# One level of Strassen's scheme in the second layer of a fused retention and feed-forward kernel

## Chip, cores and metric

The kernel runs on one core of one Trainium2 chip. Times are device microseconds of one execution. Compared runs come from the same chip, and from the same rounds, with one exception: of the seven runs of before beside e9 to e12, six are listed by the record with e1 to e4 too, so only the comparisons of e9 to e12 with each other are wholly of one call. An execution more than 1.5% above the fastest of its kernel is called slow and left out of ratios. Engines: PE is TensorE, PEld its weight loads, DVE VectorE, ACT ScalarE, POOL GpSimd.

## The reference

```python
# q, k, v: (8, 8, 576, 64)   w_in: (512, 2048)   w_out: (2048, 512), all float32
scores = (q @ k^T) / sqrt(64)
gamma  = 1 - 2 ** (-5 - arange(8))                   # per head
ret    = (scores * D) @ v     # D[i, j] = gamma ** (i - j) if i >= j else 0
x      = ret.transpose(0, 2, 1, 3).reshape(4608, 512)
h      = x @ w_in
out    = maximum(0.01 * h, h) @ w_out                # (4608, 512) float32
```

## The kernel before

Retention runs in units of up to 128 tokens, one "step" per unit: scores, outputs of the unit before, masks, states. The feed-forward part runs in token groups, three of 256, seven of 512, one of 256. `run` interleaves the first layer of group g with the second layer of group g-1 and puts the steps between their blocks. Every engine executes its instructions in the order of these calls.

```python
    def steady(n):
        def go():
            ...
            scores(n)                 # PE
            outputs(n - 1)            # PE, then ACT copy "own", then DVE sums into xT
            masks(n)                  # DVE
            states(n)                 # DVE, then POOL cast of the states
            casts(n + 2)              # ACT k, POOL q and v, DMA transpose
    ...
    def g2_blocks(g, width=1):        # second layer, 64 products of 512 columns per 512 tokens
        ...
            for f in range(4 * part, 4 * part + 4):
                for tb in tbs:
                    nc.tensor.matmul(out=y_cur[g, tb],
                        lhsT=g_tiles[g][:, f, tb * P : (tb + 1) * P],
                        rhs=w_out16[:, f, :], start=(f == 0), stop=(f == NF - 1))
            if part == 3:             # DVE copy to SBUF, then DMA out
        ...
    def run(upto, *lists):
        order = sorted(((n + 0.5) / len(ls), x, n)
                       for x, ls in enumerate(lists) for n in range(len(ls)))
        a = done
        for m, (_, x, n) in enumerate(order):
            lists[x][n]()
            run_steps(min(upto, a + -(-(upto - a) * (m + 1) // max(1, len(order) - 3)), done + 1))
        run_steps(upto)
    ...
    run(ends[3], g1[2] + g2_blocks(2))
    run(ends[4], g1_blocks(3))
    for g in range(4, NG):
        run(ends[g + 1], g1_blocks(g), g2_blocks(g - 1))
    run(ends[NG], g2_blocks(NG - 1))
```

## Time and profile before

| | before |
|---|---|
| median of its first three runs | 337.44 us (335.61 to 338.17) |
| span of the profiled run, granted clock | 337.3 us, 0.973 |
| PE, DVE, ACT, POOL busy | 299.5, 147.8, 135.6, 122.0 us |

Two rows of the groups by cost, from the page of the kernel before. The columns are busy us and mean ns of one instruction, then the idle time of the engine before them and what ended it.

```profile
L451 PE MATMUL yps<-w_out,gt 128*128 128x512 f16 x512 | 127.9, 379 | 0.0
L461 DVE COPY osb<-yps 128x512 f32<-128x512 f32 x32 | 21.9, 687 | 69.9 <-PE yps L451 69.9
```

The second layer's PE work never waits (0.0), and DVE spends most of its time before these copies idle. The mean of 379 ns is a pipelined duration; the pace is read start to start.

### The profile page before, as it was taken

What the parts mean: (1) busy time and instruction counts of PE and PEld (TensorE: products, weight loads), DVE (VectorE), ACT (ScalarE), POOL (GpSimd) and SP (SyncE); (2) the same over time, 40 slices, a digit from 0 to 9 for tenths busy, and PEclk for the clock granted to TensorE, in tenths of its full rate; (3) what the DMA queues carried; (4) which work ended last, traced back from release to release, by engine and by line L of the source; (5) the groups of instructions that cost most, each with busy time, mean ns of one, the idle gap of its engine ahead of it and who ended that gap; (6) DMA issues with size and microseconds to landing.
All of it is one profiled execution on the core that took longest, in us unless ns stands there. A gap on an engine that the chain in (4) does not pass through costs nothing.

```text
span 337.3 us, 8449 instructions
## 1 busy us (share of the span) xinstructions
PE 299.5 (89%) x3578; PEld 154.7 (46%) x3578; DVE 147.8 (44%) x326; ACT 135.6 (40%) x240; POOL 122.0 (36%) x148
## 2 busy tenths in 40 slices
PE   1798887595775699999999999999999999999995
PEld 0476643263332344444444444444444444445652
DVE  2670444945564336434453556354436553101011
ACT  3355631164153454444453545444444433332220
POOL 8786745605355333530540355035413510000000
PEclk9999799989997779999999999999999999999999
DMA  7999999879999986866779599968697211000111
GB/s 175 214 194 189 228 231 178 197 150 176 165 244 198 162 161 142 175 144 165 160 139 192 130 189 210 217 148 158 149 214 109 66 47 61 35 33 31 62 64 62
DMA packets 122982, 50.32 MB, mean 149 GB/s; under 512 B 112192, under 2 KB 116288, under 8 KB 122944
## 3 DMA queue, kind: packets, MB, share of 16 engines
q1 hardware_dynamic: 115632, 37.11, 54.8%
q0 software_dynamic: 7024, 12.59, 19.6%
q8 instruction: 28, 0.46, 0.6%
q10 hardware_dynamic: 288, 0.08, 0.1%
q14 instruction: 10, 0.08, 0.1%
HBM read 36.78 MB, written 9.44 MB: 137 GB/s over the span
## 4 chain that ended last, share of the span: by engine, by line
PE 65%; DMA 13%; issue 10%; POOL 9%; SPq 1%; DVE 0%; POOLq 0%
PE yps L451 31%; PE hps L428 29%; DMA t<-in_v_dram 6%; DMA w_out<-in_moe_w_out_dram 5%; POOL t L122 3%; POOL v L160 2%; POOL qk L140 2%; DMA qkT<-qk 2%; PE sc L201 2%; POOL w_in L343 2%; PE ot L313 1%; PE ot L303 1%; PE sc L211 1%; SPq L122 1%; SPq L148 0%
## 5 line engine op out<-in xcount | busy, mean ns | idle before, releaser
L428 PE MATMUL hps<-xT,w_in 128*128 128x512 f16 (+1 forms) x704 | 151.2, 352 | 3.6 <-DVE osb L505 3.4
L435 ACT ACTIVATE gt<-hps 128x512 f16<-128x512 f32 x144 | 85.6, 596 | 128.0 <-PE hps L428 127.8
L451 PE MATMUL yps<-w_out,gt 128*128 128x512 f16 x512 | 127.9, 379 | 0.0
L428 PEld LDWEIGHTS <-w_in 128*128 128x128 f16 x704 | 68.8, 101 | 62.7 <-issue 9.6
L327 DVE TENSOR_TENSOR xT<-ot,own 64x256 f16<-64x256 f32 (+1 forms) x144 | 50.3, 388 | 85.8 <-ACT own L321 85.3
L451 PEld LDWEIGHTS <-gt 128*128 128x128 f16 x512 | 49.1, 98 | 56.4
L249 POOL CAST st<-s 128x512 f16<-128x512 f32 x25 | 15.3, 610 | 135.3 <-DVE s L243 68.6
L461 DVE COPY osb<-yps 128x512 f32<-128x512 f32 x32 | 21.9, 687 | 69.9 <-PE yps L451 69.9
L321 ACT COPY own<-ot 128x512 f32<-128x512 f32 (+1 forms) x36 | 19.4, 538 | 38.2 <-PE ot L313 34.8
L140 POOL TENSOR_TENSOR qk<-t,cs 128x512 f16<-128x512 f32 (+1 forms) x32 | 33.4, 1043 | 0.1
L160 POOL TENSOR_TENSOR v<-t,cs 128x512 f16<-128x512 f32 (+1 forms) x32 | 33.4, 1042 | 0.0
L221 DVE TENSOR_TENSOR s<-sc,cs 128x512 f16<-128x512 f32 (+1 forms) x40 | 27.5, 689 | 5.0 <-PE sc L211 4.0
L139 ACT CAST qk<-t 128x512 f16<-128x512 f32 (+1 forms) x40 | 24.7, 620 | 7.4 <-DMA t<-in_k_dram 7.4
L201 PE MATMUL sc<-qkT 64*64 64x64 f16 x576 | 13.5, 205 | 14.6 <-DMA qkT<-qk 11.2
L201 PEld LDWEIGHTS <-qkT 64*64 64x64 f16 x576 | 9.0, 113 | 30.5 <-DMA qkT<-qk 17.2
L182 PE MATMUL yps<-ident,qk 128*128 128x128 f16 (+1 forms) x48 | 5.9, 274 | 11.3 <-ACT qk L139 8.4
L140 DVE TENSOR_TENSOR qk<-t,cs 128x512 f16<-128x512 f32 (+1 forms) x8 | 7.9, 986 | 18.0 <-DMA t<-in_q_dram 18.0
L313 PE MATMUL ot<-qkT,st 64*64 64x64 f16 x456 | 11.8, 197 | 2.2 <-ACT st L249 1.6
L303 PE MATMUL ot<-s,v 64*64 64x64 f16 x512 | 11.7, 197 | 0.3 <-DVE s L221 0.3
L122 POOL DMA_DIRECT2D t<-in_q_dram x12 | 10.5, 877 | 3.8 <-DVE qk L140 1.9
L122 POOL DMA_DIRECT2D t<-in_v_dram x12 | 10.2, 851 | 4.3 <-DMA t<-in_k_dram 1.5
L182 PEld LDWEIGHTS <-qk 128*128 128x128 f16 (+1 forms) x56 | 4.4, 119 | 16.1 <-ACT qk L139 11.1
(42 smaller groups left out, 152.8 us busy)
## 6 DMA issues: line engine op xcount, KB each, us to landing
out_dram<-osb SPq DMA_DIRECT2D x36, 256.0 KB, 2.3
t<-in_k_dram SPq DMA_DIRECT2D x23, 256.0 KB, 3.8
t<-in_q_dram SPq DMA_DIRECT2D x22, 256.0 KB, 4.5
t<-in_v_dram SPq DMA_DIRECT2D x22, 256.0 KB, 4.8
t<-in_q_dram POOLq DMA_DIRECT2D x10, 256.0 KB, 7.8
t<-in_v_dram POOLq DMA_DIRECT2D x10, 256.0 KB, 8.2
t<-in_k_dram POOLq DMA_DIRECT2D x9, 256.0 KB, 8.0
w_in<-in_moe_w_in_dram POOLq DMA_DIRECT2D x16, 128.0 KB, 6.0
```

The source lines that it names most:

```text
L122: eng.dma_start(out=t[0:n], in_=(q, k, v)[x][b, :, P * w : P * w + n, :].rearrange("h t d -> t h d"),)
L139: nc.scalar.copy(out=t[0:n, 1], in_=t32[u, 1][0:n])
L140: (nc.vector if u < NEARLY else nc.gpsimd).tensor_tensor(out=t[0:n, 0], in0=t32[u, 0][0:n], in1=tab_sb[0:n, w % 2, 0, :].unsqueeze(2).to_b ...
L160: (nc.vector if u < NEARLY else nc.gpsimd).tensor_tensor(out=t[0:n], in0=t32[u, 2][0:n], in1=tab_sb[0:n, w % 2, 1, :].unsqueeze(2).to_broa ...
L201: nc.tensor.matmul(out=a[half(j), g, 0, p, :], lhsT=qkT[u][half(g), 1, p, half(j)], rhs=qkT[u][half(g), 0, p, half(j)], start=True, stop=T ...
L221: nc.vector.tensor_tensor(out=s16s[u][0:n], in0=sc_tiles[u][0:n, :, 0], in1=mask_sb[0:n].unsqueeze(1).unsqueeze(1).to_broadcast([n, 2, NP, ...
L321: nc.scalar.copy(out=tmp[:, :, 0:nb, :], in_=own[:, 0:nb].rearrange("q j p t -> q p j t"))
L327: nc.vector.tensor_tensor(out=xT[half(o), ps, t0 : t0 + n].rearrange("q p (j t) -> q p j t", t=CH), in0=far[half(o), o ^ c, :, 0:nb, :], i ...
L428: nc.tensor.matmul(out=hps[:, f, :], lhsT=w_in16[:, c, fc * P : (fc + 1) * P], rhs=xT[:, c, t0 % XR : t0 % XR + tok], start=(c == 0), stop ...
L435: nc.scalar.activation(out=g_tiles[g][:, fb * nf : (fb + 1) * nf, :], in_=hps, func=mybir.ActivationFunctionType.Lrelu,)
L451: nc.tensor.matmul(out=y_cur[g, tb], lhsT=g_tiles[g][:, f, tb * P : (tb + 1) * P], rhs=w_out16[:, f, :], start=(f == 0), stop=(f == NF - 1),)
L461: nc.vector.tensor_copy(out=osb, in_=y_cur[g, tb])
```

## The change

The intent is to remove PE work where PE is the bound. A 512 by 2048 by 512 product is cut in two along each dimension. Seven half-size products replace eight, and sums of activations, weights and results are computed instead, all f16 sums on VectorE. Per group: four f16 sums of 2048 elements per partition, 112 products of 256 columns, five PSUM sums on DVE and two copies on ACT. Four weight sums come once.

```diff
+    def mix_weights(eng):
+        pairs = ((w_part(0, 1), w_part(0, 0)), (w_part(1, 1), w_mix[:, 0]),
+                 (w_part(1, 1), w_part(0, 1)), (w_part(1, 0), w_mix[:, 1]))
+        for n, (x, y) in enumerate(pairs):
+            eng.tensor_tensor(out=w_mix[:, n], in0=x, in1=y, op=SUB)
+    def g2_seven(g):
+        ...
+        def mix(n):
+            z, x, y, op = (
+                (s[:, 0], part(1, 0), part(1, 1), ADD),
+                (s[:, 1], s[:, 0], part(0, 0), SUB),
+                (part(1, 0), part(0, 0), part(1, 0), SUB),
+                (part(0, 1), part(0, 1), s[:, 1], SUB),
+            )[n]
+            nc.vector.tensor_tensor(out=z, in0=x, in1=y, op=op)
+        plan = (
+            ("p1", g_(0, 0), w_part(0, 0), True, lambda: keep("k1", "p1")),
+            ("p6", s(1), w_mix[:, 1], True, lambda: keep("u2", "p6", "k1")),
+            ("p1", g_(0, 1), w_part(1, 0), False, lambda: give(0, 0, "p1")),
+            ("p5", s(0), w_mix[:, 0], True, lambda: keep("v", "p5", "u2")),
+            ("p7", g_(1, 0), w_mix[:, 2], True, lambda: give(1, 1, "p7", "v")),
+            ("p5", g_(0, 1), w_part(1, 1), False, lambda: give(0, 1, "p5", "u2")),
+            ("p7", g_(1, 1), w_mix[:, 3], False, lambda: give(1, 0, "p7", "u2")),
+        )
+        def block(n, half):
+            name, lhs, rhs, fresh, then = plan[n]
+            if n == 0 and not half:
+                mix(0)
+                mix(1)
+            if n in (1, 3) and not half:
+                mix((n + 3) // 2)
+            product(name, lhs, rhs, fresh, half)       # 8 products of 256 columns
+            if half:
+                then()                                 # DVE sum or ACT copy out of PSUM
     ...
     run(ends[3], g1[2] + g2_blocks(2))
+    mix_weights(nc.vector)
     run(ends[4], g1_blocks(3))
     for g in range(4, NG):
-        run(ends[g + 1], g1_blocks(g), g2_blocks(g - 1))
+        run(ends[g + 1], g1_blocks(g), g2_seven(g - 1))
```

(Cut: buffers and smaller rings for the retention tiles. The `product`, `keep` and `give` helpers are only named.)

More of the change, by code (lines that the diff above doesn't have):

```diff
@@ L13 @@
 ADD = mybir.AluOpType.add
+SUB = mybir.AluOpType.subtract
 PSUM = bass.MemoryType.PSUM
@@ L73 @@
     a_pool = ctx.enter_context(tc.tile_pool(name="ap", bufs=4))
+    b_pool = ctx.enter_context(tc.tile_pool(name="bp", bufs=2))
     g_pool = ctx.enter_context(tc.tile_pool(name="gp", bufs=2))
     o_pool = ctx.enter_context(tc.tile_pool(name="op", bufs=4))
+    o2_pool = ctx.enter_context(tc.tile_pool(name="op2", bufs=2))
+    s_pool = ctx.enter_context(tc.tile_pool(name="sp", bufs=1))
+    m_pool = ctx.enter_context(tc.tile_pool(name="mp", bufs=1))
     sc_pool = ctx.enter_context(tc.tile_pool(name="scp", bufs=1, space=PSUM))
@@ L219, in masks @@
         n = nrows[u]
-        s16s[u] = a_pool.tile([P, 2, NP, CH], F16, name="s16")
+        s16s[u] = b_pool.tile([P, 2, NP, CH], F16, name="s16")
         nc.vector.tensor_tensor(
@@ L240, in states @@
         else:
-            tmp = a_pool.tile([P, NP, CH], FP, name="stmp")
+            tmp = b_pool.tile([P, NP, CH], FP, name="stmp")
             nc.vector.tensor_tensor(out=tmp, in0=st[:, 1], in1=s32[:, 0], op=ADD)
@@ L319, in outputs @@
         t0 = (b * S + P * w) % XR
-        tmp = a_pool.tile([P, NP, 2, CH], FP, name="own")
+        tmp = b_pool.tile([P, NP, 2, CH], FP, name="own")
         nc.scalar.copy(
@@ L422, in block @@
             if fb == 0:
-                g_tiles[g] = g_pool.tile([P, NF, tok], F16, name=f"gt{tok}")
+                if g == 1:
+                    g_tiles[g] = g_tiles["both"][:, :, tok : 2 * tok]
+                else:
+                    g_tiles["both"] = g_pool.tile([P, NF, TOK], F16, name="gt")
+                    g_tiles[g] = g_tiles["both"][:, :, 0:tok]
             hps = h_pool.tile([P, nf, tok], FP, name="hps")
@@ L469, in g2_blocks, with w_part @@
         ]
+    w_mix = const_pool.tile([P, 4, NF // 2, DM // 2], F16, name="w_mix")
+    HF, HN, HT = NF // 2, DM // 2, TOK // 2
+    def w_part(a, b):
+        return w_out16[:, a * HF : (a + 1) * HF, b * HN : (b + 1) * HN]
+    def mix_weights(eng):
+        pairs = (
+            (w_part(0, 1), w_part(0, 0)),
+            (w_part(1, 1), w_mix[:, 0]),
+            (w_part(1, 1), w_part(0, 1)),
+            (w_part(1, 0), w_mix[:, 1]),
+        )
+        for n, (x, y) in enumerate(pairs):
+            eng.tensor_tensor(out=w_mix[:, n], in0=x, in1=y, op=SUB)
@@ new lines, in g2_seven, with part, product, keep @@
+    def g2_seven(g):
+        t0 = starts[g]
+        gt = g_tiles[g]
+        r = {}
+        def part(a, b):
+            return gt[:, b * HF : (b + 1) * HF, a * HT : (a + 1) * HT]
+        def mix(n):
+            if "s" not in r:
+                r["s"] = s_pool.tile([P, 2, HF, HT], F16, name="mix")
+            s = r["s"]
+            z, x, y, op = (
[5 more added lines that the diff above has]
+            nc.vector.tensor_tensor(out=z, in0=x, in1=y, op=op)
+        def product(name, lhs, rhs, fresh, half):
+            if fresh and not half:
+                r[name] = y_pool.tile([P, 2, HN], FP, name="yps")
+            for f in range(HF // 2 * half, HF // 2 * (half + 1)):
+                for tb in range(2):
+                    nc.tensor.matmul(
+                        out=r[name][:, tb, :],
+                        lhsT=lhs()[:, f, tb * P : (tb + 1) * P],
+                        rhs=rhs[:, f, :],
+                        start=fresh and f == 0 and tb == 0,
+                        stop=f == HF - 1,
+                        skip_group_check=True,
+                    )
+        def keep(name, of, plus=None):
+            r[name] = m_pool.tile([P, 2, HN], FP, name=name)
+            if plus is None:
+                nc.scalar.copy(out=r[name], in_=r[of])
+            else:
+                nc.vector.tensor_tensor(out=r[name], in0=r[of], in1=r[plus], op=ADD)
+        def give(a, b, of, plus=None):
+            if ("o", a) not in r:
+                r["o", a] = o2_pool.tile([P, 2, DM], FP, name="osb2")
+            to = r["o", a][:, :, b * HN : (b + 1) * HN]
+            if plus is None:
+                nc.scalar.copy(out=to, in_=r[of])
+            else:
+                nc.vector.tensor_tensor(out=to, in0=r[of], in1=r[plus], op=ADD)
+            r["n", a] = r.get(("n", a), 0) + 1
+            if r["n", a] == 2:
+                r0 = t0 + a * HT
+                nc.sync.dma_start(
+                    out=out[r0 : r0 + HT, :].rearrange("(t p) d -> p t d", p=P),
+                    in_=r["o", a],
+                )
+        def s(n):
+            return lambda: r["s"][:, n]
+        def g_(a, b):
+            return lambda: part(a, b)
+        plan = (
[6 more added lines that the diff above has]
+            ("p7", g_(1, 1), w_mix[:, 3], False, lambda: give(1, 0, "p7", "u2")),
+        )
+        def block(n, half):
[8 more added lines that the diff above has]
+                then()
+        return [lambda n=n, half=half: block(n, half) for n in range(7) for half in range(2)]
```

## The prediction

> **What bounds the kernel now.** I read the busy table and the 40 slices first, then busy time in stretches, then the instructions in order of time of TensorE (PE), VectorE (DVE) and GpSimd (POOL) round a group boundary.
>
> ```profile
> PE   1798887595775699999999999999999999999995
> PEclk9999799989997779999999999999999999999999
> ```
>
> ```profile
> 80.00:120.00 40.00, 27.23 (x477) 13.16 (x478) 21.74 (x53) 14.85 (x27) 16.86 (x19) 0.89 1.24 193
> 120.00:285.00 165.00, 165.00 (x1975) 78.14 (x1974) 79.96 (x183) 74.80 (x132) 55.62 (x63) 1.00 0.71 148
> ```
>
> The columns of the second view are stretch, length, then busy us of PE, weight load, DVE, ACT, POOL, clock, DMA share, GB/s. From 120 us on PE is never idle, at clock 1.00; DVE is at 80 of 165 us (48%). So a microsecond less of PE work there is a microsecond of span, and a microsecond of new PE waiting costs the same. From 80 to 120 us PE is idle 12.8 us and the bound is a chain of waits. All seven changed second layers lie after about 124 us; the preparation of the weights lies in the chain-bound stage.
>
> The price of the two product shapes is in the last groups, PE in order of time:
>
> ```profile
> 306.35 1.04 PE L428 MATMUL hps<-xT,w_in 128*128 128x256 f16 x8
> 307.22 1.89 PE L451 MATMUL yps<-w_out,gt 128*128 128x512 f16 x8
> 308.95 1.04 PE L428 MATMUL hps<-xT,w_in 128*128 128x256 f16 x8
> ```
>
> Start to start, eight 256-column matmuls take 0.87 us (0.109 each), eight 512-column ones 1.73 us (0.216 each). Halving the columns halves the time: the 98 ns weight load of each still hides.
>
> The second thing to see is how late DVE runs after each retention step (scores, masks, states of one 128-token unit). PE, DVE and POOL at one group boundary:
>
> ```profile
> 153.59 1.03 PE L428 MATMUL hps<-xT,w_in 128*128 128x512 f16 x4
> 154.54 0.32 PE L201 MATMUL sc<-qkT 64*64 64x64 f16 x16
> ...
> 155.19 1.04 PE L451 MATMUL yps<-w_out,gt 128*128 128x512 f16 x4
> ```
>
> ```profile
> 155.96 1.53 DVE L327 TENSOR_TENSOR xT<-ot,own 64x256 f16<-64x256 f32 x4 [1.48 <-ACT own L321]
> 157.52 0.69 DVE L221 TENSOR_TENSOR s<-sc,cs 128x512 f16<-128x512 f32 x1
> ...
> 159.03 0.42 DVE L243 TENSOR_TENSOR s<-stmp,cs 128x256 f32<-128x256 f32 x1
> ```
>
> ```profile
> 159.52 0.61 POOL L249 CAST st<-s 128x512 f16<-128x512 f32 x1 [8.81 <-DVE s L243]
> 160.09 1.04 POOL L140 TENSOR_TENSOR qk<-t,cs 128x512 f16<-128x512 f32 x1
> 161.09 1.04 POOL L160 TENSOR_TENSOR v<-t,cs 128x512 f16<-128x512 f32 x1
> ```
>
> The new group's first first-layer block ends on PE at 154.45 (call it E), the step's 64x64 matmuls end 0.7 later, and DVE is through with the step only at 159.45 = E + 5.0. Then POOL at once starts 2.65 us of back-to-back work. Today nobody waits for this: PE has other blocks.
>
> **What the Trainium skill says.** (1) "TensorE: Matmul & The Clock Gate", section "Wait — 56ns, not 53.3ns?": a warm matmul costs N / 2.4 GHz plus about 2.5 ns; 0.216 and 0.109 us agree. Its section "What's actually happening" says idleness of about 3.4 us halves the clock; the trace agrees in kind (below). (2) "VectorE: DVE Perf Modes", section "The perf-mode tier table (the rule you actually need)": a tensor_tensor of 2048 bf16 elements, all in SBUF, runs at 2x in 1224 ns, at 1x 2293 ns. No DVE sum of two f16 SBUF inputs is in this trace; its f32 sums of 512 take 690 ns. I take 1.22 us as an estimate from that page. (3) "SBUF — State Buffer", section "Who interferes with whom": a DVE instruction with two SBUF inputs and a GpSimd instruction that reads SBUF exclude each other, the later one blocking fully. The trace has one such meeting, and agrees:
>
> ```profile
> 61.80 3.06 DVE L140 TENSOR_TENSOR qk<-t,cs 128x512 f16<-128x512 f32 x1
> 64.78 0.68 DVE L160 TENSOR_TENSOR v<-t,cs 128x512 f16<-128x512 f32 x1
> ```
>
> ```profile
> 61.27 1.04 POOL L160 TENSOR_TENSOR v<-t,cs 128x512 f16<-128x512 f32 x1
> 62.27 1.03 POOL L140 TENSOR_TENSOR qk<-t,cs 64x512 f16<-64x512 f32 x1
> 63.27 1.03 POOL L160 TENSOR_TENSOR v<-t,cs 64x512 f16<-64x512 f32 x1
> ```
>
> A 0.69 us DVE product issued while POOL was busy ended when POOL's whole run of three was over: it took 3.06.
>
> **The change, part by part.** *PE work.* Per group 64 x 0.216 = 13.8 us become 112 x 0.109 = 12.2; 1.65 saved, times seven groups: **-12 us**, all on the path.
>
> *DVE work.* Four f16 sums of 2048 elements (4 x 1.22 = 4.9 us) and five PSUM sums for four copies (about +0.7): +5.6 us on 14 us of each group of some 29 us. DVE goes from 48% to about 67%: not the bound by throughput.
>
> *Where it waits.* The instruction order of the changed kernel (built, not run) puts, at each new group, one first-layer block, one retention step, and then on DVE the first two sums, strictly behind that step's work. The second product reads the second sum, and PE gets to it after the step and four half-blocks: E + 0.7 + 4 x 0.865 = E + 4.2. DVE is free at E + 5.0 when the step's unit has three state sums, E + 4.6 with two, E + 3.7 without states (64-row units). Two dependent sums add 2.5. So PE waits even with no contention: by the five full and two short cases, groups in order 2.9, 3.3, 2.9, 2.9, 2.0, 2.0 us, and the last, which has no step but must wait for the last activation, about 0.8. Sum **+16.8 us**.
>
> *The lock.* In the first four groups POOL is released by the same state sum, and its 2.65 us falls against the two sums. Whoever is first, the second sum depends on the first, so POOL gets in between or ahead, and by the 61.80 case keeps the port until its run ends. +2.65 each, four times: **+10.6 us**. The other groups' steps have no states, so POOL is done by then.
>
> *Weight sums.* Four sums, 4.9 us, once, on DVE ahead of a step at about 94 us, in the stage where PE already waits for DVE:
>
> ```profile
> 98.19 0.32 PE L201 MATMUL sc<-qkT 64*64 64x64 f16 x16 [2.13 <-DVE s L239]
> ```
>
> Each step there is fed by the one before (DVE states, POOL casts, DMA transpose, scores), so a delay is handed on: **+5 us**, less if the transposes catch up.
>
> *Clock.* After such idle stretches the clock sags: after 2.76 us idle the next eight 512-column matmuls took
>
> ```profile
> 105.35 3.10 PE L428 MATMUL hps<-xT,w_in 128*128 128x512 f16 x8
> ```
>
> 3.10 instead of about 1.9 in the same view, 1.2 us lost. Five waits of 5 us or more: up to 6; I put **+3**.
>
> *The rest.* The product buffers are freed by DVE or ACT one product or more before PE needs them; by the same count the third buffer (freed by the sum u2) is ready at about the time PE comes, so 0 to 0.4 us. Two ACT copies (1.2 us per group on 45%) and larger output transfers (DMA share 0.71) are beside other work. The smaller rings of retention buffers (two for four) are reused two steps later: no wait. Sum: 337.4 - 12 + 16.8 + 10.6 + 5 + 3 = 361.
>
> **The rivals.** (a) *The saving comes through*: 337 - 12 = 325. For it: PE is the bound and DVE has 52% free. Against: the free half lies at the wrong place; it needs the sums finished 2 to 3 us earlier than DVE's order allows. (b) *The wait without the lock*: if POOL and DVE alternate or don't exclude each other, 337.4 - 12 + 16.8 + 5 + 1 = 348. For it: L243, which has two SBUF inputs, never exceeds 426 ns; against: POOL idles waiting for it then, and the one real overlap took 3.06 us. (c) *DVE sums at 1x*, 2.29 us: two more us per group and four in the weights, and DVE near 80%: about 375. Against: f16 copies of 512 from PSUM take 418 ns where f32 ones take 690, so 16-bit data does run at 2x here. (d) *Narrow matmuls cost more than half*: refuted by the 0.87 us rows.
>
> **Range and chances.** I weigh the full sum (361) at about 0.65, (b) (348) at 0.2, the slow sums at 0.05 and at 0.1 some slack that I don't see (330 to 340). That gives 357, with 8 in 10 between 344 and 369. Faster by over 2% (under 330.7) needs nearly all waits to be hidden: 0.05; within 2%: 0.09; slower: 0.86.
>
> **What would show it.** Right: 784 matmuls of 256 columns at 0.109 us start to start; each group's second product waiting on PE for the DVE sum named mix, 2 to 3 us in the fifth and sixth group and 5 to 6 us in the first four; a mix sum (or POOL's cast) of 3 to 4 us instead of 1.2 beside POOL work; scores near 98 us moved by about 5; clock digits below 9 after 120 us. Wrong: no wait on mix (then the order or the durations are misread and (a) holds), sums of 2.3 us (c), sums of 1.2 us with POOL running beside them (b), or a wait at the buffers of the products instead.

## The result and the profile after

The changed kernel took 350.84 us (median of five, 347.67 to 354.8) against 337.43 us for the kernel before (335.61 to 338.17). The ratio is 1.0349, 95% interval 1.0294 to 1.0403: slower. A ratio here comes from the fast runs alone, so it is not quite the ratio of the medians, which are over all runs. Repeated later in other rounds (e9_after_again) it took 350.29 against 336.42, ratio 1.0419 (1.0347 to 1.0491). The first profile of the changed kernel fell in a slow run (353.0 us, clock 0.942), so I read the fast profile of that repetition: 349.1 us, clock 0.966, against 337.3 us, 0.973. (In the runs listed with both, the span is some 1.8 us below the time. So the profiled run of before stands for about 339.1 us, 1.7 above its median, and the two profiles differ by less than the medians do.)

From the page of the changed kernel, the slices that answer to those of before:

```profile
PE   1787987774837596998799799979997997999995
PEclk9999898999978898999899999999999999999999
```

The unbroken row of nines of before now has a dent at the start of each group. PE in order of time at the first changed group, and DVE and POOL in the same stretch:

```profile
127.04 1.05 PE L522 MATMUL yps<-w_out,gt 128*128 128x256 f16 x8
...
129.66 1.03 PE L437 MATMUL hps<-xT,w_in 128*128 128x512 f16 x4
133.75 1.78 PE L522 MATMUL yps<-w_mix,mix 128*128 128x256 f16 x8 [3.06 <-DVE mix L515]
135.33 1.91 PE L437 MATMUL hps<-xT,w_in 128*128 128x512 f16 x4
```

```profile
127.97 1.53 DVE L332 TENSOR_TENSOR xT<-ot,own 64x256 f16<-64x256 f32 x4 [4.22 <-ACT own L326]
...
130.59 0.42 DVE L244 TENSOR_TENSOR s<-sc,s 128x256 f32<-128x256 f32 x1
130.93 1.21 DVE L515 TENSOR_TENSOR mix<-gt 128x2048 f16<-128x2048 f16 x1
132.18 1.51 DVE L515 TENSOR_TENSOR mix<-mix,gt 128x2048 f16<-128x2048 f16 x1
133.61 2.06 DVE L515 TENSOR_TENSOR gt<-gt 128x2048 f16<-128x2048 f16 x1
```

```profile
131.08 1.54 POOL L254 CAST st<-s 128x512 f16<-128x512 f32 x1 [4.65 <-DVE s L244]
132.58 2.01 POOL L145 TENSOR_TENSOR qk<-t,cs 64x512 f16<-64x512 f32 x1
134.55 2.02 POOL L165 TENSOR_TENSOR v<-t,cs 64x512 f16<-64x512 f32 x1
```

PE idles 3.06 us until the second sum is done. That sum waits for the first, and the first stands behind the retention step's work on DVE. After the wait, eight narrow products take 1.58 us start to start instead of 0.87, so the clock has sagged (granted clock 0.52 from 133.75 to 137.20 us, 1.00 just before). DVE and POOL take turns: each sum after the first waits for one POOL operation, and each POOL operation for one sum (the cast 1.54 instead of 0.61 us).

In the table of waits, with total, count and longest in us:

```profile
PE yps L522 <- DVE mix L515: 15.2, 7, 3.4
PE sc L206 <- DVE s L244: 6.9, 2, 6.7
```

The first row is seven waits of 3.06, 3.41, 2.22, 2.18, 1.88, 1.83 and 0.59 us. The second is nearly all one wait of 6.7 us, just after the weight sums; the same wait was 2.13 us before. Those are on DVE in order of time, ahead of the step that PE's next scores need:

```profile
92.56 1.64 DVE L494 TENSOR_TENSOR w_mix<-w_out 128x2048 f16<-128x2048 f16 x1
...
97.24 1.21 DVE L494 TENSOR_TENSOR w_mix<-w_out,w_mix 128x2048 f16<-128x2048 f16 x1
98.37 1.52 DVE L332 TENSOR_TENSOR xT<-ot,own 64x256 f16<-64x256 f32 x4
```

```profile
101.55 0.43 PE L206 MATMUL sc<-qkT 64*64 64x64 f16 x16 [6.74 <-DVE s L244]
```

Two landmarks on PE cut each profile into three stretches: the start of the last 20 wide products of the third group, and the start of the second layer of the fourth, the first changed one. Lengths in us, from the starts in the timelines:

| profile | I: to landmark 1 | II: to landmark 2 | III: to the end |
|---|---|---|---|
| before (337.3) | 88.2 | 36.6 | 212.5 |
| changed, fast (349.1) | 87.0 | 40.1 | 222.1 |
| changed, slow (353.0) | 89.7 | 39.2 | 224.1 |

Stretch I has the same instructions in all (with smaller rings of buffers in the changed kernels); in the profiles it lies between 87.0 and 94.1 us, which no change explains. In the fast profile the loss of 11.8 us is -1.2 in I, +3.5 in II and +9.6 in III (rounded).

Stretch II varies too where nothing was changed: 36.6 us here and 33.9 in e6, which has the same code up to landmark 2; 37.6 to 40.1 in the seven profiles with the weight sums at their first place. The clock is a part of it. The last 24 first-layer products of the stretch, before and in e6:

```profile
116.38 7.85 PE L428 MATMUL hps<-xT,w_in 128*128 128x512 f16 x24
115.78 5.47 PE L428 MATMUL hps<-xT,w_in 128*128 128x512 f16 x24
```

The granted clock in the first was 0.67. In the fast profile of the changed kernel the same 24 took 7.04 us. So +3.5 in II is the weight sums' place and the luck of the clock together.

### The profile page after: what moved, and what is told of

It reads as the page before. It is cut to its first block, busy times and chain, and to the rows that moved or that the text cites. A ratio compares the mean times of both kernels' runs of the same rounds, so it can differ in the third digit from the quotient of the medians.

```text
span 353.0 us, 9125 instructions
## 1 busy us (share of the span) xinstructions
PE 298.6 (85%) x3914; PEld 190.9 (54%) x3914; DVE 194.8 (55%) x365; ACT 144.2 (41%) x254; POOL 139.6 (40%) x148
## 4 chain that ended last, share of the span: by engine, by line
PE 53%; DMA 12%; issue 11%; POOL 10%; DVE 10%; ACT 2%; SPq 1%; POOLq 0%; ACTq 0%
PE hps L437 26%; PE yps L522 22%; DVE mix L515 5%; DMA t<-in_q_dram 4%; POOL t L127 3%; DMA qkT<-qk 3%; DMA t<-in_k_dram 3%; POOL v L165 3%; DMA w_in<-in_moe_w_in_dram 2%; POOL qk L145 2%; DVE xT L332 2%; PE yps L460 2%; PE sc L206 2%; POOL w_in L348 1%; DVE s L226 1%
## 5 line engine op out<-in xcount | busy, mean ns | idle before, releaser
L254 POOL CAST st<-s 128x512 f16<-128x512 f32 x25 | 20.8, 833 | 133.1 <-DVE s L244 67.0
L522 PEld LDWEIGHTS <-gt 128*128 128x128 f16 x560 | 54.0, 98 | 17.4
L522 PE MATMUL yps<-w_mix,mix 128*128 128x256 f16 x224 | 31.6, 289 | 15.2 <-DVE mix L515 15.2
L522 PE MATMUL yps<-w_out,gt 128*128 128x256 f16 x336 | 43.5, 273 | 0.0
L145 POOL TENSOR_TENSOR qk<-t,cs 128x512 f16<-128x512 f32 (+1 forms) x32 | 39.5, 1233 | 0.1
L165 POOL TENSOR_TENSOR v<-t,cs 128x512 f16<-128x512 f32 (+1 forms) x32 | 39.2, 1224 | 0.0
L522 PEld LDWEIGHTS <-mix 128*128 128x128 f16 x224 | 22.5, 104 | 25.8 <-DVE mix L515 18.4
L522 PE MATMUL yps<-w_mix,gt 128*128 128x256 f16 x224 | 28.9, 273 | 0.0
L545 DVE TENSOR_TENSOR osb<-yps,u 128x512 f32<-128x512 f32 x14 | 9.6, 689 | 23.1 <-PE yps L522 23.1
L145 DVE TENSOR_TENSOR qk<-t,cs 128x512 f16<-128x512 f32 (+1 forms) x8 | 5.5, 690 | 18.4 <-ACT gt L444 10.6
L460 PE MATMUL yps<-w_out,gt 128*128 128x512 f16 x64 | 15.6, 403 | 0.0
```

The source lines that it names most:

```text
L145: (nc.vector if u < NEARLY else nc.gpsimd).tensor_tensor(out=t[0:n, 0], in0=t32[u, 0][0:n], in1=tab_sb[0:n, w % 2, 0, :].unsqueeze(2).to_b ...
L165: (nc.vector if u < NEARLY else nc.gpsimd).tensor_tensor(out=t[0:n], in0=t32[u, 2][0:n], in1=tab_sb[0:n, w % 2, 1, :].unsqueeze(2).to_broa ...
L254: (nc.scalar.copy if u < NEARLY else nc.gpsimd.tensor_copy)(out=st16[u], in_=s32)
L460: nc.tensor.matmul(out=y_cur[g, tb], lhsT=g_tiles[g][:, f, tb * P : (tb + 1) * P], rhs=w_out16[:, f, :], start=(f == 0), stop=(f == NF - 1),)
L522: nc.tensor.matmul(out=r[name][:, tb, :], lhsT=lhs()[:, f, tb * P : (tb + 1) * P], rhs=rhs[:, f, :], start=fresh and f == 0 and tb == 0, s ...
```

## The experiments

The theory: PE pays for the place of the first two sums on DVE, and for the weight sums. The rivals: the work of the sums or the DVE/POOL lock, the narrow products, the clock.

**e1_sums_early.** The first two sums are issued before the group's first step.

```diff
-            if n == 0 and not half:
-                mix(0)
-                mix(1)
 ...
+        mix(0)
+        mix(1)
         return [lambda n=n, half=half: block(n, half) ...]
```

> The first two sums of each group are issued on VectorE ahead of the group's first retention step, all else as in the changed kernel. Theory (TensorE waits for the second sum because it stands behind the step's work): the seven waits on mix, 15.2 us of idle TensorE in the profile of the changed kernel, go, and with them the half-clock stretches after them; 350.8 falls to 330 to 336. Rival (the lock between VectorE and GpSimd or the added VectorE work is the cost, wherever the sums stand): under 5 us gained, 345 or more.

Measured: 335.15 us, ratio to before 0.9975 (0.9905 to 1.0045). This before took 336.42. Most of the loss is gone, as the theory said. Its profile fell in a slow run (339.8 us, stretches 94.0, 39.1, 206.8), so only its waits and stretch III are used. The waits of PE:

```profile
PE ot L318 <- POOL st L254: 3.2, 4, 1.0
PE yps L522 <- DVE mix L515: 0.6, 1, 0.6
```

The seven waits on mix have become one of 0.6 us, and stretch III, though of a slow run, is 15.3 us shorter than in e9. A smaller one has appeared: the third sum still starts together with POOL's cast of the states, delays it by 0.9 us, and PE waits for that cast.

**e2_weights_late.** The weight sums move behind the stage of first layers.

```diff
-    mix_weights(nc.vector)
     run(ends[4], g1_blocks(3))
+    mix_weights(nc.vector)
```

> The four weight sums are moved behind the stage with first layers alone, where VectorE idles; all else as in the changed kernel. Theory (they delay a chain of waits by some 5 us that isn't made up): scores wait near 104 us (6.6 us) shrinks to about 2 and the time falls by 4 to 6 us, 345 to 347. Rival (the chain catches up through the transposes): under 2 us.

Measured: 351.66 us, ratio 1.0471 (1.0384 to 1.0558). Nothing was gained, as the rival said, but not for its reason. Stretch II shrank from 40.1 to 33.4 us, and III grew from 222.1 to 227.4. DVE in order of time, and PE:

```profile
123.72 2.06 DVE L494 TENSOR_TENSOR w_mix<-w_out,w_mix 128x2048 f16<-128x2048 f16 x1
125.70 1.52 DVE L332 TENSOR_TENSOR xT<-ot,own 64x256 f16<-64x256 f32 x4
...
128.65 1.22 DVE L515 TENSOR_TENSOR mix<-gt 128x2048 f16<-128x2048 f16 x1
```

```profile
131.47 1.89 PE L522 MATMUL yps<-w_mix,mix 128*128 128x256 f16 x8 [6.84 <-DVE mix L515]
```

The weight sums now delay the first group's step and with it the first two sums: that wait became 6.84 us. The cost was handed from one chain to the next.

**e3_both.** Both moves together.

> Both moves. Theory: they add up, only the 12 us of saved TensorE work is left, 325 to 331. Rival (one wait takes the other's place): 333 or more.

Measured: 335.64 us, ratio 0.9988 (0.9905 to 1.0071). The rival is right: one wait takes the other's place. Stretch II was 33.6 us, III 213.2. PE in order of time:

```profile
128.65 1.05 PE L522 MATMUL yps<-w_mix,mix 128*128 128x256 f16 x8 [3.61 <-DVE mix L515]
```

The late weight sums fall into the first group again.

**e4_no_wait.** A wrong result: the second product reads plain activations, all sums stay.

```diff
-            ("p6", s(1), w_mix[:, 1], True, ...
+            ("p6", g_(1, 1), w_mix[:, 1], True, ...
```

> Wrong result on purpose: the second product reads activations in place of the second sum, so that TensorE doesn't wait for it, while every sum is still computed at its place. Theory: 330 to 336, as with the sums issued early, so that it is the waiting and not the work of the sums or the lock that costs. Rival: 345 or more.

Measured: 335.88 us, ratio 1.0001 (0.994 to 1.0063). The sums, their place and the DVE/POOL turns are all still there; only PE's dependence on the second sum is gone, and with it 15 us of median time. So the wait is the larger part of the loss, not the sums' work. What the sums' work and the turns can cost beside it is bounded by stretch III: 207.5 us, 5.4 above that of e5, the next run.

**e5_no_sums.** Wrong: all activation and weight sums are left out.

```diff
-            nc.vector.tensor_tensor(out=z, in0=x, in1=y, op=op)
+            pass
 ...
-    mix_weights(nc.vector)
```

(The `plan` rows that named sums read plain parts.)

> Wrong result on purpose: the changed kernel with all sums of activations and weights left out, the seven products and their PSUM sums kept. Theory (only the sums' place on VectorE costs; the products save 1.66 us in each of seven groups): 337 - 12 = 325, between 322 and 328, and TensorE waits for nothing in the second layers. Rival (the narrow products, their weight loads or the PSUM sums cost as well): 331 or more.

Measured: 328.14 us, ratio 0.9732 (0.9673 to 0.9791), just above the 322 to 328 that the theory expected and below the rival's 331. Stretch III is 202.1 us, 10.4 less than before; II is 36.0. Busy time in a stretch (columns as in the prediction):

```profile
120.00:300.00 180.00, 179.68 (x2402) 118.52 (x2401) 89.41 (x201) 90.67 (x159) 55.63 (x63) 1.00 0.71 145
```

PE is without waits again, at full clock. This is the floor for the scheme in this kernel. The PSUM sums, the ACT copies, the larger output transfers and the smaller rings are all still in this run, so none of them is the reason for the loss.

**e6_narrow.** The kernel before with each wide product of the seven groups cut into two narrow ones.

```diff
-                    nc.tensor.matmul(out=y_cur[g, tb], lhsT=..., rhs=w_out16[:, f, :],
+                    for h in range(2 if sizes[g] == TOK else 1):
+                        hs = slice(h * 256, h * 256 + 256) if sizes[g] == TOK else slice(0, DM)
+                        nc.tensor.matmul(out=y_cur[g, tb][:, hs], lhsT=..., rhs=w_out16[:, f, hs],
```

> The kernel before with each 512-column product of the seven groups cut into two of 256 columns, nothing else: 128 narrow matmuls and weight loads in place of 64. Theory (a narrow one costs 0.109 us, half of a wide one, its weight load hidden): 0.2 us per group more, the time within 1% of before. Rival (weight loads show at this width): 5 us or more slower.

Measured: 338.61 us against 337.53, ratio 1.0044 (0.9973 to 1.0114). Stretch III was 213.6 us against 212.5. Twice the number of products and weight loads costs some 1 us: narrow products are not the reason.

**e7_warm_wait and e12_warm_six.** The changed kernel with eight matmuls of zeros in the waits, in all seven groups and then in the first six.

```diff
+            if n == 1 and not half:            # e12: and g < 9
+                keep_warm(8)
             product(name, lhs, rhs, fresh, half)
```

> The changed kernel with eight matmuls of zeros (1.7 us) ahead of each second product, where TensorE waits 0.6 to 3.4 us for the sum: the wait stays, most of the idleness goes. Theory (part of the loss is the clock that sags after idle stretches: eight narrow matmuls took 1.3 to 1.7 us instead of 0.87 after some waits): 344 to 348 against 350.8, granted clock at least 0.01 higher. Rival (the sag is not caused by these waits, or too rare to matter): 351 to 353, as the last group's short wait makes it 1.1 us longer.

> The changed kernel with eight matmuls of zeros in the waits of the first six groups alone (the last group's wait is too short for them). Theory (the sag of the clock after the waits costs 3 to 5 us): 345 to 348, 3 to 5 us less than e9_after_again. Rival (the clock sags about as often without these waits, so that filling them gives nothing, as the earlier attempt with seven suggests): within 1.5 us of e9_after_again.

Measured: e7 350.32 us, ratio 1.0367 (1.0291 to 1.0442). That alone says little, because the changed kernel did not run beside it (stretch III of its profile is 219.3 us, 2.7 less than in e9). With five rounds beside each other, e12 took 347.03 us (345.98 to 348.16) and the unchanged e9 350.29 (347.91 to 352.2), ratios to the same kernel before 1.0333 (1.0284 to 1.0383) and 1.0419. The intervals overlap a little; the medians differ by 3.3 us. PE in e12, in order of time:

```profile
130.37 1.89 PE L367 MATMUL hps<-idle 128*128 128x512 f16 x8
133.49 1.05 PE L522 MATMUL yps<-w_mix,mix 128*128 128x256 f16 x8 [1.23 <-DVE mix L515]
134.37 1.03 PE L437 MATMUL hps<-xT,w_in 128*128 128x512 f16 x4
```

Work that computes nothing makes the kernel faster: the wait is as long (1.89 us of zeros and 1.23 idle), but the narrow products after it run in 0.88 us. Stretch III is 218.4 us, 3.7 less than in e9. So filling the waits brings back about 3 us, which I take for the clock's part of the loss. It is shown in the traces and only just separated in the times.

**e8_spread and e11_spread_again.** A version that tries to keep the saving: first two sums early, third sum at the third product, weight sums in two pairs where DVE has room.

```diff
-            if n == 0 and not half:
-                mix(0)
-                mix(1)
-            if n in (1, 3) and not half:
-                mix((n + 3) // 2)
+            if n in (2, 3) and not half:
+                mix(n)
+            if g == 3 and n == 3 and not half:
+                mix_weights(nc.vector, 2, 4)
 ...
+        mix(0)
+        mix(1)
         return [...]
 ...
-    mix_weights(nc.vector)
-    run(ends[4], g1_blocks(3))
+    fc = g1_blocks(3)
+    fc[8] = lambda f=fc[8]: (f(), mix_weights(nc.vector, 0, 2))
+    run(ends[4], fc)
```

> From the run with the first two sums issued early: the third sum goes from beside GpSimd's cast to the third product, two weight sums to VectorE's idle time after a step of the stage before, the other two into the first group after its fourth sum. Theory (what is left over no sums is GpSimd's delayed cast, some 3 us, and the weight sums' chain, some 5 us): 326 to 331, faster than the kernel before by over 2%. Rival (the rest of the loss lies in the noisy first 120 us or in the added VectorE work): 333 or more.

> The kernel of e8_spread unchanged, for an interval: 328 to 332, ratio to the kernel before 0.975 to 0.985. If the earlier 0.980 was luck, 0.99 or more.

Measured: 330.72 us, ratio 0.9796 (0.973 to 0.9863), then with five rounds 330.39, ratio 0.9832 (0.9771 to 0.9892). The result is correct. It beats both kernels: the kernel before by 1.7 to 2.0%, with both intervals below 1 (whether the gain is over 2% stays unclear), the changed one by some 20 us. The profile of e8 fell in a slow run, so that of e11 is read. Waits of PE after 118 us in e11:

```profile
PE sc L206 <- DVE s L226: 1.3, 1, 1.3
PE sc L206 <- DMA qkT<-qk: 1.0, 2, 0.8
PE sc L206 <- DVE s L244: 0.6, 1, 0.6
PE yps L522 <- DVE mix L515: 0.6, 1, 0.6
```

3.5 us of waits are left of more than 15. Stretches: 87.1, 33.7, 206.0.

**e9_after_again and e10_weights_back.** The first is the changed kernel repeated, reported above. The second is e8 with the weight sums back at their first place, nothing else.

> The changed kernel once more, beside the three below on one chip: 348 to 352, about 1.035 times the kernel before, unless the first measurement was a matter of the chip. Wanted too: a profile in the fast state, where the waits on mix should again be some 15 us in seven places.

> The run e8_spread with the four weight sums put back at their place in the changed kernel, nothing else. Theory (there they delay a chain of waits by 3 to 5 us, measured between the last wide second-layer block of the third group and the first narrow product: 38 to 39 us against 33 to 36.6 without them): 3 to 5 us slower than e11_spread_again. Rival (they are hidden, and moving the third sum was what helped): within 1 us of it.

Measured, same rounds as e11: e10 334.13 us, ratio 0.9934 (0.9863 to 1.0004), 3.7 us above e11's median. Its stretch II is 37.8 us against 33.7. That is the price of the weight sums' first place against the two places of e11, of which the second lies in stretch III (206.0 us in e11, 204.9 in e10).

## Why the prediction was right, and where a step was off

The direction, the class and the range were right: 350.8 us lies between 344 and 369. The centre, 357, was 6 us too high. The case held most likely, 361 at 0.65, did not come; the measured time is nearer to rival (b), 348 at 0.2, and the range held both.

1. *PE work, -12.* Measured -10.4 in stretch III (e5 against before). The mechanism holds; e6 accounts for about 1 us, as twice the narrow products cost 1.1 us there.
2. *The wait at the second product, +16.8 without the lock.* This was the main step, and it held: 15.2 us in seven places, 14.0 without the lock. The size by group was predicted as 2.9, 3.3, 2.9, 2.9, 2.0, 2.0, 0.8 and measured as 3.06, 3.41, 2.22, 2.18, 1.88, 1.83, 0.59. The third and fourth are shorter because the unit whose outputs are summed there has 64 rows, which I overlooked (its four xT sums take about 1.0 us instead of 1.53, and the ACT copy before them 0.37 instead of 0.59). e1 and e4 show that this wait makes most of the loss.
3. *The lock, +10.6.* This step failed. The prediction said that POOL "keeps the port until its run ends". DVE and POOL do exclude each other, but they take turns: the second sum lost 0.29 us (1.51 against 1.22) in each of four groups, 1.2 in all, and POOL paid most of it. No run takes the lock away alone; 1.2 us is read off the trace. I had carried over one case, the f32 product of 3.06 us at 61.80. That case is real and recurs: in other profiles the same instruction took up to 4.20 us and mostly ended after POOL's whole run. But it is no rule for f32 either. In e11 DVE got in ahead of POOL's last operation (e4 shows the same):

```profile
60.21 3.08 DVE L145 TENSOR_TENSOR qk<-t,cs 128x512 f16<-128x512 f32 x1
63.22 1.52 DVE L165 TENSOR_TENSOR v<-t,cs 128x512 f16<-128x512 f32 x1
```

```profile
61.70 1.04 POOL L145 TENSOR_TENSOR qk<-t,cs 64x512 f16<-64x512 f32 x1
62.70 1.49 POOL L165 TENSOR_TENSOR v<-t,cs 64x512 f16<-64x512 f32 x1
```

Why the f32 products waited for several POOL operations and the f16 sums for one is open.
4. *Weight sums, +5.* Measured 3.5 (stretch II, clock included) and 3.7 us (e10 against e11); the wait of the scores grew by 4.6 us, from 2.13 to 6.74. The step held.
5. *Clock, +3.* Measured about 3 us (e12), on two of the seven waits in the fast profile, both over 3 us. The size is partly luck: it was put for five waits of 5 us or more, and none was over 3.41.
6. *Rivals.* (c) falls: the sums take 1.21 to 1.23 us uncontended, not 2.29. (By its own terms, 14 for seven groups and 4 for the weights on top of 361, it should have read 379, not 375.) (d) falls by e6. (b), at 348, was the nearest: a wait with hardly any lock.

Put together for the fast profile, in us: -10.4 (products) + 15.2 (waits on mix, lock included) + 3.5 (stretch II: weight sums and clock, against this run of before) + 3.2 (slow work after the waits that end at 133.75 and 167.76, start to start) + 1.5 not assigned in III - 1.2 (stretch I, no cause) = 11.8.

## What to carry to other kernels

When work moves from the bound engine to one with free time, ask when in that engine's own order the result comes, not how much time it has free: here DVE went from 44% to 56% busy and the kernel lost 13 us, and moving a few calls turned that into a gain of 6. A delay in a chain is not removed by moving its cause to the next chain (e2). And a contention seen once, for one instruction form, gives no size for another form.

## What the Trainium skill lacked or had wrong

- "SBUF — State Buffer", section "Who interferes with whom", says that the second to issue is blocked until the first finishes. It does not say who is next when both queues have work. Here f16 sums and POOL operations alternated (sums 1.21, 1.51 and 2.06 us, cast 1.54, products 2.01 and 2.02), while an f32 product with two SBUF inputs mostly waited through to the end of a run of POOL operations (3.06 us before, 4.20 in e12, instead of 0.69), and in e4 and e11 got in ahead of the last of them.
- "TensorE: Matmul & The Clock Gate", section "Back-to-back issue gap", gives about 131 ns per 512-column matmul as a sustained rate in a stream of weight loads and matmuls. Here such a stream ran at 216 ns, and 256 columns at 109 ns, which is the formula that the page calls isolated.
- The same page, section "What's actually happening", gives an idle window of about 3.4 us, free-running, before the clock halves. In the fast profile, waits of 3.06 and 3.41 us were followed by narrow products at 1.58 and 1.46 us for eight instead of 0.87, and the waits of 2.22 us and less were not. But no threshold comes out of the runs: after a wait of 3.42 us in the first profile of the changed kernel the eight took 0.89 us, after 3.61 us in e3 0.88 (the clock sagged one block later), and after 2.19 us in e2 1.38.
- No page has the value of filler work: eight matmuls of zeros in each wait went with 3.3 us less (350.29 to 347.03).
